# Layer 1's third and fourth quarters as seven half-size products, layer 2's first operands made just ahead of use

## The chip, the cores and the metric

The kernel runs on one core of a Trainium2 chip. The metric is device microseconds (us) of one execution. One execution was also taken with the hardware profiler, and all stretches and waits below come from it.

Five engines work side by side, each on its own list of instructions in order: PE (matrix products, whose weight loads are listed as PEld), DVE and ACT (element-wise work, both can read the products' banks), POOL (element-wise work on SBUF alone) and SP, which here only issues DMAs. An instruction waits until the semaphores that it names have been raised.

## What is computed

Retention attention, then two feed-forward layers on the 2304 tokens that it gives. The attention part is the same before and after, and is left out here:

```python
def _moe_ref(x, w_in, w_out) -> np.ndarray:
    h = x @ w_in
    g = np.maximum(0.01 * h, h)
    return (g @ w_out).astype(np.float32)
...
def _moe2_ref(x, w_in, w_out) -> np.ndarray:
    h = x @ w_in
    alpha = 1.0
    g = np.where(h > 0.0, h, alpha * (np.exp(np.minimum(h, 0.0)) - 1.0))
    return (g @ w_out).astype(np.float32)
...
    x = _moe_ref(x=x, **moe_kwargs)
    return _moe2_ref(x=x, **moe2_kwargs)
```

Tokens are 2304 = 4 blocks of 512 and a small one of 256; the model width is 512, the inner width 2048. Weights arrive as 64-bit floats, and 32-bit accuracy is kept by splitting each operand into a high and a low part and taking three products: high x high, low x high, high x low.

## The kernel before

**The tiling.** Each layer goes through four quarters of the inner width (`q`, 512 wide, four slices `f` of 128). In a quarter the four blocks of 512 tokens are taken one after the other, then the small one. For a block a quarter has a *first product* (x by `w_in`, into banks `ps_h`), the activation, and a *second product* (the result `g` by `w_out`, into four banks `ps_y`), which is added to `yp` in SBUF. A second product is always 4 slices x 4 banks x 3 = 48 matmuls of 512 columns, in four parts of 12, one part for a slice.

**Layer 1, all four quarters.** The first product is plain (`moe_h`): 4 slices x 4 x 3 = 48 matmuls of 512 columns. The work is a list of units (quarter, block, slice); a loop runs over it and takes the second product of a unit three units later (`LAG`). Beside them it splits the weights of the next quarter (`split_a`, `split_b`, `split_c`: two instructions on ACT, four on DVE, then a copy on ACT and a subtraction on DVE or POOL). The table `turn` says at which unit, from 54 on, what else is done.

**Layer 2, all four quarters.** The first product of a block is made as seven half-size ones (`seven`, `seventh`; Strassen's scheme in Winograd's form): 7 x 12 = 84 matmuls of 256 columns, called P1, P2, P5, P3, P6, P7, P4 in their order. Their operands are sums of quarters of x (four tiles for each block, `k` = 0 to 3, name `xo` when loaded back from DRAM and `xs` when just made, always high and low part) and sums of quarters of the weights (`ws`, made on POOL by `sums_a` and `sums_b`). P1, P6, P7 and P4 add into one bank (called `a` in the code), P2 has its own, P5 and P3 share one. Between them the results are read: a copy of a bank by ACT (`k1`, `k5`, `k3`, tile `cc`), then an addition of another bank to it by DVE (`c1`, `c2`, `c3`, tile `c`). So P6 needs `k1` to have read bank `a`, P7 needs `c2`, and P4 needs `c3`. Each of the four results then goes through five steps (ACT, ACT, DVE, ACT copies the high part, DVE subtracts it to get the low part, into `gg`).

The order of all this within a block is a string of tokens, one for each engine's next step (`ORDER`):

```python
        "turn": (
            "f0 P1 k1 aa P2 f1 c1 P5 k5 1 1 ba ba ba ba y s ga 1 ab 1 w P3 f2 k3 P6 c2 1 da 2 2 "
            "bb bb 2 y 2 P7 f3 c3 2 3 3 bb 2 y bb db s s gb 3 P4 4 4 3 4 go y s"
        ),
```

`P` is one of the seven products; `y` is the next waiting part of a second product, here that of the block before, the last `y` the block's own first part; `1` to `4` are the next step of one of the four activations; `f` loads an operand of the next block from DRAM; `a`, `b`, `d` with a letter are the steps of splitting a weight slab; `s` is a step of `stage`; `w` makes a `ws` tile.

**Between the layers.** `stage(blk)` makes the operands of layer 2 out of `yp`: seven high parts on ACT, seven low parts and four differences on DVE, and it sends four tiles to DRAM. Blocks 0 to 2 are staged inside layer 1's last quarter, from units 60, 64 and 70 on, and loaded back; block 3 is staged in layer 2's first blocks and its tiles are used directly.

Of the kernel before, what the change touches and what calls it, by code (L numbers as in the profile page):

```python
# [15 lines left out]
ALU = mybir.AluOpType  # L16
# [20 lines left out]
LAG = 3  # L37

# [15 lines left out]
def _in_order(y, parts):  # L54

    for k in (parts, 1, 1):
        y = y.reshape(k, -1, 2, DM).transpose(0, 2, 1, 3).reshape(-1, DM)
    return y
# [33 lines left out]
def retention_moe(  # L92
# [257 lines left out]
    def split_a(key):  # L350
# [3 lines left out]
        if key[0] == "i" and FT <= key[1] < FT + FQ:  # L354
            u = bpool.tile([P, DM], F32, tag="c", name="u", bufs=6)
        else:
            u = dpool.tile([P, DM], F32, tag="u", name="u", bufs=2)
# [22 lines left out]
    def split_c(key):  # L380

        u = words[key]
        if key[0] == "o" or key[1] < FT or key in added:
            del words[key]
# [4 lines left out]
        engine = nc.gpsimd if key[1] < FQ or key[1] >= FT and key not in early else nc.vector  # L389
# [21 lines left out]
    def moe_h(u):  # L411
# [5 lines left out]
        for i, f in enumerate(fs):  # L417
# [8 lines left out]
            for k, (a, x) in enumerate(ops):  # L426
                product(h[:, i * n : (i + 1) * n], a, x, start=k == 0, stop=k == len(ops) - 1)
# [142 lines left out]
    def evac(m, q, blk, cols, y):  # L570
# [3 lines left out]
        for e in range(len(y)):  # L574
# [12 lines left out]
    units = [  # L587
        (0, q, blk, fs)
        for q in range(NQ)
        for blk in ([0, 1, NMAIN, 2, 3] if q == NQ - 1 else range(NB))  # L590
        for fs in ([(f,) for f in range(FQ)] if blk < NMAIN else [(0, 1), (2, 3)])
    ]
    nsteps = B * STEPS
# [4 lines left out]
        for kind, k in zip(*(("ioioiioo", (0, 0, 1, 1, 2, 3, 2, 3)) if i < FT else ("ooiiiioo", (0, 2, 0, 1, 2, 3, 1, 3))))  # L598
    ]
    early = [("o", FT), ("o", FT + 2)]  # L600
    late = "i16 i17 o14 o15 i18 i19 o16 o18"
    late = [(k[0], int(k[1:])) for k in late.split()]
    at = order.index(("o", FT - 2))
    order = order[:at] + late + order[at + 8 :]
# [13 lines left out]
    def may_split(n):  # L618
# [4 lines left out]
        return i < WB or last_use[kind, min(i, FT + 1) - WB] <= n + (kind == "i")  # L623
# [3 lines left out]
    spilled, operands = {}, {}  # L627

    def stage(blk):

        a = yp.pop(blk)
        assert blk not in yb
# [4 lines left out]
        def room(k, ops=2):  # L637
            where = (big, "big") if blk >= NMAIN - 2 and k % 2 == 0 else (xpool, "x")
            kept[k] = where[0].tile([P, ops, 2, 2, n], F32R, tag=where[1], name="xs")
# [14 lines left out]
        def send(k):  # L654
            t = kept.pop(k)
            d = spill.tile(list(t.shape), F32, tag=f"x{blk}{k}", name=f"x{blk}{k}")
            nc.sync.dma_start(out=d, in_=t.bitcast(F32))
            spilled[blk, k] = d
            if blk == NMAIN - 1:
                operands[blk, k] = t  # L660
# [9 lines left out]
        yield from pair(0, b11, b21)  # L670
        t1 = less(b12, b11)
        yield
        send(0)
        yield from pair(1, t1, b22)
        t2 = less(b22, t1)
        t3 = less(b22, b12)
        yield
        send(1)
        yield from pair(2, t2, t3)
        t4 = less(b21, t2)  # L680
        yield
        send(2)
        yield from pair(3, t4)
        yield
        send(3)
# [22 lines left out]

    def sums_b(key):
        i = key[1]  # L710
        for j in (i, i + 1):
            added.add(("i", j))
            if ("i", j) in weights:
                del words["i", j]
        t = sums[i]
# [9 lines left out]
    def seventh(out, q, blk, j, first=False):  # L725

        n = SIZES[blk] // 2
        x = operands[blk, j // 2][:, j % 2]
        for pair in range(2):
            i = FT + q * FQ + 2 * pair  # L730
# [7 lines left out]
            for kk in range(2):  # L738
                c = slice(kk * P, (kk + 1) * P)
                for a, b in ((0, 0), (1, 0), (0, 1)):  # L740
# [4 lines left out]
                    )  # L745

# [19 lines left out]
    def second_y(q, blk, gg):  # L766

        n = SIZES[blk]
        y = yb[blk] = [bank("y", 4) for _ in range(n // P)]
        order = (0, 2, 1, 3)  # L770
        for f in order:
            wh, wl = weights["o", FT + q * FQ + f]
            gh, gl = (gg[f % 2][:, k, f // 2] for k in range(2))
            for e in range(n // P):
                g = slice(e * P, (e + 1) * P)
                ops = (gh[:, g], wh), (gh[:, g], wl), (gl[:, g], wh)
                for k, (a, x) in enumerate(ops):
                    product(y[e], a, x, start=f == 0 and k == 0, stop=f == FQ - 1 and k == 2)
            if f == FQ - 1:
                evac(1, q, blk, DM, yb.pop(blk))  # L780
            yield

    def small_y(q, gg):
        blk, n = NMAIN, SMALL
        y = yb[blk] = [bank("y", 4) for _ in range(n // P)]
# [446 lines left out]
```

## Time and profile before

| what | value |
|---|---|
| three runs | 809.67, 812.0 and 812.81 us, median 812.0 |
| the profiled execution's own time | 808.98 us |
| its span, first to last instruction | 807.2 us |
| PE, busy share of the span | 99% |
| PE clock granted, in every 20 us but the last | 1.00 |
| DVE, ACT, POOL busy share | 66%, 55%, 19% |

The attention fills the first 140 us or so, together with the first quarter of layer 1; layer 1 goes on to about 438 us, and layer 2 fills the rest. The 1.8 us between the span and the execution's own time lie outside the first and last instruction. Of the views, the page shares out the span by engine, the chain of waits lists what the end was waiting for, piece by piece, the timeline lists instructions in order of time with the idle time ahead of each and what ended it, and the windows give the busy time of each engine in a stretch.

### The profile page before, as it was taken

To read this page: it belongs to the slowest core of one execution; us is meant where nothing else is said; L and a number is where in the kernel's file an instruction comes from. 1 tells how busy PE (TensorE), PEld (TensorE's weight loads), DVE (VectorE), ACT (ScalarE), POOL (GpSimd) and SP (SyncE) were. 2 spreads that over 40 slices of the span, in tenths; PEclk is the share of its full clock that TensorE was granted. 3 is DMA by queue.
4 is the path that set the end of the run, shared out by engine and by line. 5 is a ranking of instruction groups with operands and counts; after the bars stand their busy time and mean duration, and the time that the engine had idled before them with its cause. 6 is when DMAs were issued, how large, how long until landed. Compare 5 with 4: busy or idle time off the path is not lost.

```text
span 807.2 us, 13312 instructions
## 1 busy us (share of the span) xinstructions
PE 795.8 (99%) x5240; PEld 711.2 (88%) x5240; DVE 535.6 (66%) x879; ACT 444.3 (55%) x755; POOL 156.0 (19%) x142
## 2 busy tenths in 40 slices
PE   8899999999999999999999999999999999999998
PEld 5778888888888888888889999999999999999997
DVE  5998962556234762568797788557785877775444
ACT  3465534574234542445666688677675766565442
POOL 2566441000000000004121113221134113410000
PEclk9999999999999999999999999999999999999999
DMA  8994530122001220113369976526663565445512
GB/s 337 329 341 142 193 90 14 53 74 62 23 3 49 79 79 0 43 38 105 94 245 369 397 277 236 233 104 247 248 240 134 222 272 212 175 153 182 213 54 78
DMA packets 34094, 129.97 MB, mean 161 GB/s; under 512 B 4080, under 2 KB 7408, under 8 KB 26736
## 3 DMA queue, kind: packets, MB, share of 16 engines
q1 hardware_dynamic: 33744, 128.99, 44.4%
q8 instruction: 41, 0.67, 0.3%
q14 instruction: 21, 0.17, 0.1%
q10 hardware_dynamic: 288, 0.14, 0.1%
HBM read 109.71 MB, written 19.40 MB: 160 GB/s over the span
## 4 chain that ended last, share of the span: by engine, by line
PE 88%; DMA 3%; issue 3%; DVE 2%; POOL 1%; ACT 1%; SPq 0%; DVEq 0%; POOLq 0%; ACTq 0%
PE ps_y L409 44%; PE ps_h L409 41%; DMA ain<-in_att 2%; PE ps_h L214 1%; PE ps_h L260 1%; DMA raw<-in_moe_out 1%; DMA kn<-in_att 1%; PE ps_h L307 0%; PE ps_h L272 0%; DVE raw L370 0%; POOL wil L390 0%; DVE ain L232 0%; DVE u L377 0%; DVE xt L291 0%; ACT u L358 0%
## 5 line engine op out<-in xcount | busy, mean ns | idle before, releaser
L409 PE MATMUL ps_y<-woh,gg 128*128 128x512 f32 x580 | 183.7, 378 | 0.0
L439 DVE TENSOR_TENSOR gl<-g,gh 128x512 fp32r<-128x512 f32 x64 | 44.7, 699 | 117.4 <-ACT g L433 117.2
L409 PEld LDWEIGHTS ps_y<-woh,gg 128*128 128x128 f32 x580 | 109.7, 190 | 13.5
L432 ACT ACTIVATE gh<-ps_h 128x512 fp32r<-128x512 f32 x64 | 38.3, 598 | 145.1 <-PE ps_h L409 145.0
L409 PE MATMUL ps_y<-gh,woh 128*128 128x512 f32 x288 | 110.8, 385 | 0.4 <-ACT woh L388 0.3
L409 PE MATMUL ps_y<-wol,gg 128*128 128x512 f32 x290 | 109.6, 378 | 0.0
L409 PE MATMUL ps_y<-gl,woh 128*128 128x512 f32 x288 | 109.3, 380 | 0.0
L409 PE MATMUL ps_y<-gh,wol 128*128 128x512 f32 (+1 forms) x288 | 106.1, 368 | 0.7 <-POOL wol L390 0.7
L409 PE MATMUL ps_h<-xh,wil 128*128 128x512 f32 x256 | 97.4, 380 | 1.9 <-POOL wil L390 1.9
L409 PE MATMUL ps_h<-xh,wih 128*128 128x512 f32 x256 | 97.5, 381 | 1.3 <-ACT wih L388 1.0
L409 PEld LDWEIGHTS ps_h<-xo,ws 128*128 128x128 f32 x720 | 86.2, 192 | 1.9 <-DVE c L852 0.4
L409 PE MATMUL ps_h<-xo,ws 128*128 128x256 f32 x720 | 87.8, 275 | 0.0
L390 POOL TENSOR_TENSOR wil<-u,wih 128x512 fp32r<-128x512 f32 x20 | 25.6, 1287 | 295.6 <-ACT wih L388 295.5
L409 PE MATMUL ps_h<-xl,wih 128*128 128x512 f32 x256 | 65.7, 379 | 0.0
L409 PE MATMUL ps_h<-xo,wih 128*128 128x256 f32 x360 | 65.1, 275 | 0.0
L409 PEld LDWEIGHTS ps_y<-gh,woh 128*128 128x128 f32 x288 | 54.5, 189 | 9.1 <-ACT woh L388 1.0
L409 PEld LDWEIGHTS ps_y<-gh,wol 128*128 128x128 f32 x288 | 54.6, 190 | 8.5 <-POOL wol L390 1.1
L852 DVE TENSOR_TENSOR c<-ps_h,cc 128x512 f32<-128x512 f32 x48 | 33.1, 690 | 42.9 <-PE ps_h L409 32.1
L579 DVE TENSOR_TENSOR yp<-yp,ps_y 128x512 f32<-128x512 f32 x96 | 59.7, 685 | 2.4 <-PE ps_y L409 2.4
L409 PEld LDWEIGHTS ps_y<-gl,woh 128*128 128x128 f32 x288 | 54.5, 189 | 7.0
L409 PEld LDWEIGHTS ps_y<-wol,gg 128*128 128x128 f32 x290 | 55.1, 190 | 5.7
L358 ACT ACTIVATE u<-raw 128x512 f32<-128x512 f32 x64 | 54.0, 844 | 9.9 <-DMA raw<-in_moe_in 6.6
(117 smaller groups left out, 1492.7 us busy)
## 6 DMA issues: line engine op xcount, KB each, us to landing
xo<-x SPq DMA_DIRECT2D x45, 1024.0 KB, 6.6
raw<-in_moe_in SPq DMA_DIRECT2D x32, 512.0 KB, 3.5
raw<-in_moe_out SPq DMA_DIRECT2D x32, 512.0 KB, 3.6
x<-xs SPq DMA_DIRECT2D x12, 1024.0 KB, 6.6
ain<-in_att SPq DMA_DIRECT2D x16, 512.0 KB, 6.8
xo<-x SPq DMA_DIRECT2D x15, 512.0 KB, 4.6
ain<-in_att SPq DMA_DIRECT2D x20, 256.0 KB, 7.5
out<-yp SPq DMA_DIRECT2D x17, 256.0 KB, 2.1
```

The source lines that it names most:

```text
L214: nc.tensor.matmul(sc[j][keys[j], pr * n : (pr + 1) * n], t[r, 1, pr * n : (pr + 1) * n], t[r, 0, pr * n : (pr + 1) * n], start=True, stop ...
L260: nc.tensor.matmul(x[half[j], pr * n : (pr + 1) * n], st[b][:, j, pr, :], t[:, 2 * j, pr * n : (pr + 1) * n], start=pr == 0, stop=n < CH, ...
L358: nc.scalar.activation(u, high.bitcast(F32), AF.Abs, scale=2.0**16)
L390: engine.tensor_tensor(l, u, h.bitcast(F32), ALU.subtract)
L409: nc.tensor.matmul(out, w, x, **flags)
L432: nc.scalar.activation(gh, h, AF.Prelu, alpha=0.01)
L439: nc.vector.tensor_tensor(gl, g, gh.bitcast(F32), ALU.subtract)
L579: nc.vector.tensor_tensor(t, t, y[e], ALU.add)
L852: nc.vector.tensor_tensor(t, x, y, ALU.add)
```

## The change

Layer 1's first two quarters stay as they are, as 36 units. Its third and fourth quarter now go through `seven`, as layer 2 does, with the activation `prelu` (ACT, then the high part by ACT and the low part by DVE) in the place of `elu`. Their operands are made by a new function, `stage_first`, during the second quarter: for each block it adds the high and low part of x together again on DVE, takes four differences, splits these into high and low parts, and sends seven operands, each in two parts, to DRAM, 14 DMAs of 256 KB a block. The table `turn` starts at unit 16 now.

Layer 2's operands are no longer staged inside layer 1's last quarter for blocks 0 to 2. Each block's `stage` runs one block ahead of its use: that of block 0 in layer 1's last block (kind `last`), those of blocks 1, 2 and 3 in layer 2's first three blocks (kinds `next`, `turn`, `turn`). The tiles are used directly, and also sent to DRAM for the later quarters. In layer 1's last quarter the small block stands second. Every kind of block has a new token string. `split_c` puts the subtraction of layer 2's first three `i` and `o` slabs on DVE. The columns of `moe_h`'s products are paired in another pattern, and the host puts the rows back accordingly.

```diff
@@
-        engine = nc.gpsimd if key[1] < FQ or key[1] >= FT and key not in early else nc.vector
+        engine = nc.gpsimd if key[1] < FQ or key[1] >= POOLED else nc.vector
@@
-                product(h[:, i * n : (i + 1) * n], a, x, start=k == 0, stop=k == len(ops) - 1)
+                product(h[:, i * n : (i + 1) * n], a, x, 2, start=k == 0, stop=k == len(ops) - 1)
@@
+        if q == NQ - 1 and m == 0:
+            stages.append(stage(blk))
+    PLAIN = 2
     units = [
         (0, q, blk, fs)
-        for q in range(NQ)
-        for blk in ([0, 1, NMAIN, 2, 3] if q == NQ - 1 else range(NB))
+        for q in range(PLAIN)
+        for blk in range(NB)
@@
+    def stage_first(blk):
...
+        def whole(j, t):
+            a = bpool.tile([P, 2, n], F32, tag="c", name="a", bufs=6)
+            h, l = (part(x, j, t).bitcast(F32) for x in (xh, xl))
+            nc.vector.tensor_tensor(a, h, l, ALU.add)
+            return a
...
+        def high(k, x):
+            made[k] = bpool.tile([P, 2, n], F32R, tag="t", name="xs", bufs=3)
+            nc.scalar.activation(made[k], x, AF.Copy)
+
+        def low(k, x, *at):
+            h = made.pop(k)
+            l = bpool.tile([P, 2, n], F32R, tag="t", name="xs", bufs=3)
+            nc.vector.tensor_tensor(l, x, h.bitcast(F32), ALU.subtract)
+            for p, t in enumerate((h, l)):
+                nc.sync.dma_start(out=to[at[0]][:, at[1], p], in_=t.bitcast(F32))
...
@@
+    def prelu(c, g, j, cut):
         t = bpool.tile([P, DM], F32, tag="t", name="t", bufs=3)
-        nc.scalar.activation(t, c, AF.Relu, scale=-1.0)
-        yield
-        nc.scalar.activation(t, t, AF.Exp, scale=-1.0)
-        yield
-        nc.vector.scalar_tensor_tensor(t, t, -1.0, c, ALU.add, ALU.max)
+        nc.scalar.activation(t, c, AF.Prelu, alpha=0.01)
...
@@
+        "last": (
+            "s P1 k1 P2 e P5 k5 s s c1 1 w ga 1 y 1 s 1 P3 p P6 k3 c2 2 1 2 y s P7 s 2 c3 2 2 2 3 "
+            "y w s gb P4 4 3 3 go 4 y 3 4 s"
+        ),
+        "next": (
+            "s P1 k1 e aa s P2 c1 P5 ba s k5 1 ba ba 1 s ab y ba 1 P3 k3 ga 1 P6 c2 1 da 2 bb 2 2 "
+            "bb s 2 P7 c3 2 3 y 3 bb 2 s s bb y db 3 P4 4 gb 4 3 4 go s y"
+        ),
+        "turn": (
+            "s s P1 k1 aa P2 c1 P5 s k5 1 ba ba ba ba ga 1 y ab 1 s P3 1 k3 P6 c2 da 2 2 bb s 1 "
+            "bb 2 y P7 c3 s bb 2 3 bb 2 gb y s db 2 3 3 P4 4 4 p go y s 4 3"
+        ),
...
@@
+            for blk in ((0, NMAIN, 1, 2, 3) if (m, q) == (0, NQ - 1) else range(NB))
...
+            (0, 2): ("regular", "regular", "regular", "hold", "small"),
+            (0, 3): ("head", "head", "bring", "last", "third"),
+            (1, 0): ("next", "turn", "turn", "hold", "small"),
```

On PE, in layer 2's first block from P5 on (`ws` products are P5, P3, P6 and P7; the second product's parts stand as rows of `woh` and `wol`). Before:

```order
L409 MATMUL ps_h<-xo,ws 128x256 x24
L409 MATMUL ps_y<-gh,woh 128x512
L409 MATMUL ps_y<-gl,woh 128x512
L409 MATMUL ps_y<-gh,wol 128x512
...
L409 MATMUL ps_h<-xo,ws 128x256 x12
```

And now:

```order
L408 MATMUL ps_h<-xs,ws 128x256 x12
L408 MATMUL ps_y<-gg,woh 128x512 x2
L408 MATMUL ps_y<-gg,wol 128x512
...
L408 MATMUL ps_h<-xs,ws 128x256 x36
L408 MATMUL ps_y<-gg,woh 128x512 x2
L408 MATMUL ps_y<-gg,wol 128x512
```

Before, P3 and P6 (24 matmuls) were followed by a part of the second product and only then by P7 (12); now P3, P6 and P7 stand in one row of 36.

On DVE, in layer 2's second block from `c3` on (`c` is the addition of a bank, `gg` a low part of an activation, `xs` a low part and `t<-yp,t` a difference of `stage`, `u` a weight slab being put together). Before:

```order
L852 TENSOR_TENSOR c<-ps_h,cc 128x512
L760 TENSOR_TENSOR gg<-t,gg 128x2x256
L375 SCALAR_TENSOR_TENSOR u<-u,raw 128x512
L377 ISA u<-u,last 128x1024
L645 TENSOR_TENSOR xs<-t,xs 128x512
L645 TENSOR_TENSOR xs<-yp,xs 128x512
```

And now:

```order
L943 TENSOR_TENSOR c<-ps_h,cc 128x512
L711 TENSOR_TENSOR xs<-t,xs 128x512 x2
L717 TENSOR_TENSOR t<-yp,t 128x512
L374 SCALAR_TENSOR_TENSOR u<-u,raw 128x512
L376 ISA u<-u,last 128x1024
L838 TENSOR_TENSOR gg<-t,gg 128x2x256
```

The low part of the second activation stood right behind `c3`; now three steps of `stage` and two of a weight slab stand between them.

## Rows read from the trace of the kernel before

**Rows 1.** The page: busy time by engine, then the chain's shares

```profile
PE 795.8 (99%) x5240; PEld 711.2 (88%) x5240; DVE 535.6 (66%) x879; ACT 444.3 (55%) x755; POOL 156.0 (19%) x142
PE 88%; DMA 3%; issue 3%; DVE 2%; POOL 1%; ACT 1%; SPq 0%; DVEq 0%; POOLq 0%; ACTq 0%
```

**Rows 2.** Chain of waits, pieces: start us, length us, what, matmuls

```profile
271.01 2.59 PE ps_h L409 x12
...
567.25 4.02 PE ps_h L409 x36
571.27 2.59 PE ps_y L409 x12
573.86 2.68 PE ps_h L409 x24
```

**Rows 3.** Windows: stretch, length, busy us (instructions) of each engine, clock, DMA share, GB/s

```profile
146.50:376.90 230.40, 230.40 (x1115) 203.41 (x1114) 126.05 (x219) 101.09 (x177) 9.75 (x7) 1.00 0.15 49
...
437.76:457.50 19.74, 19.74 (x134) 18.48 (x132) 16.77 (x28) 12.06 (x21) 1.31 (x2) 1.00 1.01 400
457.50:477.71 20.21, 20.21 (x134) 18.46 (x132) 16.33 (x27) 17.09 (x30) 3.55 (x3) 1.00 0.93 355
...
547.35:567.09 19.74, 19.74 (x134) 18.46 (x132) 14.22 (x23) 13.16 (x23) 3.80 (x4) 1.00 0.72 281
```

**Rows 4.** The page, groups: count, busy us, mean ns of one, idle before

```profile
L409 PE MATMUL ps_h<-xo,ws 128*128 128x256 f32 x720 | 87.8, 275 | 0.0
...
L409 PEld LDWEIGHTS ps_h<-xo,ws 128*128 128x128 f32 x720 | 86.2, 192 | 1.9 <-DVE c L852 0.4
```

**Rows 5.** Timeline of PE in layer 1's last quarter: start us, length us, instruction, idle before

```profile
376.30 1.03 PE L409 MATMUL ps_h<-xl,wih 128*128 128x512 f32 x4
377.67 0.48 PE L409 MATMUL ps_y<-gh,woh 128*128 128x512 f32 x1 [0.35 <-ACT woh L388]
377.99 0.38 PE L409 MATMUL ps_y<-gl,woh 128*128 128x512 f32 x1
378.40 0.48 PE L409 MATMUL ps_y<-gh,wol 128*128 128x512 f32 x1
378.72 0.38 PE L409 MATMUL ps_y<-gh,woh 128*128 128x512 f32 x1
```

**Rows 6.** Timeline of DVE in layer 2's second block: start us, length us, instruction

```profile
462.03 1.29 DVE L760 TENSOR_TENSOR gg<-t,gg 128x512 fp32r<-128x512 f32 x2
463.24 0.69 DVE L852 TENSOR_TENSOR c<-ps_h,cc 128x512 f32<-128x512 f32 x1
463.84 0.52 DVE L370 TENSOR_SCALAR raw<-raw 128x512 uint32<-128x512 uint32 x1
464.25 0.44 DVE L372 TENSOR_SCALAR u<-u 128x512 f32<-128x512 f32 x1
464.72 0.74 DVE L375 SCALAR_TENSOR_TENSOR u<-u,raw 128x512 uint32<-128x512 uint32 x1
465.60 0.69 DVE L377 CUSTOM_DVE_ANT_0 u<-u,last 128x1024 uint16<-128x1024 uint16 x1
466.21 0.68 DVE L754 SCALAR_TENSOR_TENSOR t<-t,c 128x512 f32<-128x512 f32 x1
```

**Rows 7.** The page, DMA issues: count, KB each, median us to landing

```profile
xo<-x SPq DMA_DIRECT2D x45, 1024.0 KB, 6.6
```

**Rows 8.** Timeline of all engines in the same block, around P7

```profile
468.80 0.69 DVE L852 TENSOR_TENSOR c<-ps_h,cc 128x512 f32<-128x512 f32 x1 [1.90 <-ACT cc L857]
...
469.16 0.38 PE L409 MATMUL ps_y<-woh,gg 128*128 128x512 f32 x1
469.36 1.28 POOL L390 TENSOR_TENSOR wol<-u,woh 128x512 fp32r<-128x512 f32 x1 [10.29 <-ACT woh L388]
469.40 1.78 DVE L760 TENSOR_TENSOR gg<-t,gg 128x512 fp32r<-128x512 f32 x1
...
469.54 1.41 PEld L409 LDWEIGHTS ps_h<-xo,ws 128*128 128x128 f32 x12 [0.40 <-DVE c L852]
```

More of the change, by code (lines that the diff above doesn't have):

```diff
@@ L597, in retention_moe @@
         for i in range(FQ, 2 * FT, FQ)
-        for kind, k in zip(*(("ioioiioo", (0, 0, 1, 1, 2, 3, 2, 3)) if i < FT else ("ooiiiioo", (0, 2, 0, 1, 2, 3, 1, 3))))
+        for kind, k in zip(*(("ioioiioo", (0, 0, 1, 1, 2, 3, 2, 3)) if i < PLAIN * FQ else ("ooiiiioo", (0, 2, 0, 1, 2, 3, 1, 3))))
     ]
[L600 to L604, printed above, removed]
     loads, splits = list(order), list(order)
@@ L637, in room @@
         def room(k, ops=2):
-            where = (big, "big") if blk >= NMAIN - 2 and k % 2 == 0 else (xpool, "x")
-            kept[k] = where[0].tile([P, ops, 2, 2, n], F32R, tag=where[1], name="xs")
+            kept[k] = xpool.tile([P, ops, 2, 2, n], F32R, tag="x", name="xs")
         def high(k, i, x):
@@ L779, in second_y, with small_y @@
             if f == FQ - 1:
-                evac(1, q, blk, DM, yb.pop(blk))
+                evac(m, q, blk, DM, yb.pop(blk))
             yield
-    def small_y(q, gg):
+    def small_y(m, q, gg):
         blk, n = NMAIN, SMALL
-        y = yb[blk] = [bank("y", 4) for _ in range(n // P)]
-        last = q == NQ - 1
+        parts = KC if m == 0 else n // P
+        y = yb[blk] = [bank("y", 4) for _ in range(parts)]
+        last = m == 1 and q == NQ - 1
         groups = [(0, 1), (2, 3)] if last else [(f,) for f in range(FQ)]
@@ L890, in seven @@
-    def seven(kind, q, blk, room, rounds, keep, side, begun=None):
+            "s s P1 k1 aa P2 c1 P5 s k5 1 ba ba ba ba ga 1 y ab 1 s P3 1 k3 P6 c2 da 2 2 bb s 1 "
+            "bb 2 y P7 c3 s bb 2 3 bb 2 gb y s db 2 3 3 P4 4 4 p go y s 4 3"
+        ),
+        "small": (
+            "h h h e y h w h h y e y"
+        ),
+        "third": (
+            "h aa ba ba h y ba h ab bb h h ba bb y bb da y h bb db"
+        ),
+        "end": (
+            "h h y h e e w h h y y h"
+        ),
+    }
@@ L894, in seven, with small_unit @@
+    def small_unit(kind, m, q, room, rounds, side):
+        finish()
+        slabs, ops = dict(zip("ab", rounds)), {}
+        gg = room()
+        parts = small_h(m, q, gg)
+        for token in ORDER[kind].split():
+            if token == "h":
+                go(parts, 1)
+            else:
+                beside(token, slabs, ops, side)
+        go(parts)
+        pending.append(small_y(m, q, gg))
+    def seven(kind, m, q, blk, to, room, rounds, side):
         n = SIZES[blk] // 2
-        to = (blk + 1) % NMAIN if (q, blk) != (NQ - 1, NMAIN - 1) else None
@@ L898, in seven @@
         g, banks, copies, acts, ops = [], {}, {}, {}, {}
+        act = elu if m else prelu
         def operand(x):
-            if to is not None and (q, to) != (0, NMAIN - 1):
+            if to is not None:
                 load_x(to, x)
@@ L922, in seven @@
                 y = add_up(banks["b" if x == "1" else "a"], copies.pop({"1": "1", "2": "3", "3": "5"}[x]))
-                acts[int(x)] = elu(y, g, int(x) // 3, lower if x == "1" else upper)
+                acts[int(x)] = act(y, g, int(x) // 3, lower if x == "1" else upper)
             elif op in "1234":
@@ new lines, in retention_moe @@
+        hpool = None
+        for m, q, blk in todo:
+            kind = kinds[m, q][blk]
+            rounds = [splits.pop(0) for _ in range(min(2, len(splits)))] if "aa" in ORDER[kind] else []
+            if blk == NMAIN:
+                small_unit(kind, m, q, room, rounds, side)
+                continue
+            to = blocks.index((m, q, blk)) + 1
+            to = blocks[to] if to < len(blocks) else None
+            if to and to[:2] == (1, 0):
+                to = None
+            seven(
+                kind, m, q, blk, to and to[0] * NMAIN + to[2],
+                room if hpool else first_room, rounds, side,
+            )
+            if not hpool:
+                in_first.close()
+                hpool = ctx.enter_context(
+                    tc.tile_pool(name="hpool", bufs=2, reuse_waits="tile")
+                )
```

311 lines of the change are left out of this document (186 added, 125 removed).

## The prediction

> **What bounds the kernel now.** The page comes first: PE is busy 795.8 of 807.2 us, and the chain that ends last lies to 88% on PE [rows 1]. So I look for PE time that goes and for PE waits that come. The chain's pieces give PE's pace [rows 2]: twelve matmuls of 512 columns take 2.59 us, 0.216 each, and thirty-six of 256 columns 4.02 us, 0.1117 each. The windows then show where PE has no gap at all: in layer 1's second and third quarter (230 us) it is busy for the whole stretch, with DVE at 126 us and POOL at 9.75, and the granted clock is 1.00 [rows 3]. A block of layer 2 thus needs 84 x 0.1117 + 48 x 0.2158 = 9.38 + 10.36 = 19.74 us, and two of the three blocks in the windows take 19.74 us to the hundredth; the third takes 20.21 [rows 3]. PE's pace explains the time to a hundredth wherever it doesn't wait, so the change is to be counted in matmuls and in waits.
>
> **Part 1, fewer columns on PE: -7.8 us.** Four blocks in each of two quarters change their first product from 48 matmuls of 512 columns to 84 of 256. That is 10.36 against 9.38 us, 0.98 us a block, 7.8 us over eight. The small blocks keep their columns. What a half-size matmul pays for its own weight load is in the row already: the 720 of them against `xo` have as many loads, of 192 ns each [rows 4], and still 36 follow one another in 4.02 us.
>
> **Part 2, waits of before that go: -1.4 us.** In layer 1's last quarter PE waited for the high part of a weight slab: four matmuls from 376.30 on would end at 377.16 by the pace of 0.216, and the next starts at 377.67, 0.51 late; those at 377.99, 378.40 and 378.72 come 0.10, 0.19 and 0.10 later than the pace, 0.9 us together [rows 5]. That slab is now split at other places. The second block of layer 2 took 20.21 instead of 19.74 us [rows 3], 0.47 us; its order is replaced. Sum 1.37.
>
> **Part 3, operands for layer 1: 0.** `stage_first` puts 12 DVE instructions a block into the second quarter, 48 in all. At 0.69 us, the mean of an addition of this size [rows 6], that is 33 us in a quarter of some 93 us. DVE was busy 126 of 230 us there [rows 3], 51 of 93, so it would be at 84 of 93 if none overlapped, and the activations that it delays are used three units (15.5 us) later. I take 0. If DVE lagged there by as much as all twelve instructions of a block, 8.3 us, that would still be less than those 15.5. The prelu spares one ACT instruction and one DVE instruction for each activation against `elu`, so blocks of layer 1's third and fourth quarter have a lighter DVE than those of layer 2. Their operands are loaded back on SP's queue, 1 MB in 6.6 us [rows 7]. They go into tiles that P2, P3, P7 and P4 of the block before set free; the last load is issued some 17 us into a block and lands by 24, and P4, which reads it, runs 15.8 us into the next, at 35.5. The cover is 11 us, and more than one whole load; other traffic of that stretch must eat it before PE sees it. I take 0; two uncovered landings would be 13.2 us.
>
> **Part 4, layer 2's first three blocks, new waits: +2.5 us.** Here `stage` of the next block now lies in the same blocks as the splits and activations; before, one block was staged there, now three.
> In kind `next`, P6 and P7 have become adjacent. P7 writes into the bank that `c2` reads, and `c2` needs P6's end. A half-size matmul takes 275 ns from start to end [rows 4] and the next starts after 112, so 0.16 us of drain; then `c2` for 0.69 us, and 0.05 us until P7's weight load starts (`c2` at 468.80, load at 469.54 [rows 8]). That is 0.9 us, once. Before, a part of the second product stood there and hid it.
> In kind `turn`, two blocks, the block's own first part of the second product needs the low part of activation 2. PE comes there after 84 half-size products and 36 of 512 columns, 9.38 + 7.77 = 17.15 us into the block. P7 ends at 72 x 0.1117 + 24 x 0.2158 = 13.22, with the drain 13.4. On DVE stand from there `c3`, three steps of `stage`, the two of the weight slab, then the low part. From starts in [rows 6]: an addition or subtraction occupies DVE for 0.60 us (463.24 to 463.84), the slab's addition 0.88 (464.72 to 465.60), the custom step 0.61; the low part itself takes 0.69. So 13.4 + 4 x 0.60 + 0.88 + 0.61 + 0.69 = 17.98, and PE waits 0.83 us, twice 1.65. Together 2.5 us. The lower end is 0, if the profile's spacing hides a part of DVE's queue; the upper follows from the next part.
>
> **Part 5, DVE beside POOL: +1.6 us.** A low part on DVE took 1.78 us where it began 0.04 us after POOL's subtraction of 1.28 us [rows 8]; alone two such take 1.29 together [rows 6]. So a collision costs 1.09 us of DVE. In the three blocks POOL has ten instructions (two, two, and two with four sums of weights), and the windows of before show three to four instructions of POOL at most in such a block [rows 3]. DVE has no slack to take them: kind `next` has 35 DVE instructions, 27 at 0.60 and 8 of a split at 4.4 together, 20.6 us in a block of 19.74; `turn` has 30, 17.6 us, where before 27 and 28 were busy for 16.3 and 16.8 [rows 3]. The block that I read closely has one collision; I take one in each of the three blocks, and half of their 3.3 us reaching PE, 1.6. The ends are 0 and all ten, 10.9 us.
> [...]
>
> **The sum.** -7.8 - 1.4 + 2.5 + 1.6 = -5.1 us. The profiled execution took 808.98 us, of which 1.8 us lie outside the span; it lies 3.0 us below the median of the three runs. I put the change on both alike: 803.9 us for an execution like the profiled one, 806.9 us against the median of 812.0.
>
> **The rivals.**
> *The whole gain.* DVE keeps up in the three blocks and the new waits stay near 0: -7.8 - 1.4 = -9.2, 802.8 us. For it: the lag at the first part of the second product is 0.8 us, close to nothing. Against it: P7's wait behind P6 has nothing to hide it.
> *Layer 2's turn eats most of it.* DVE carries its lag from `next` into the first `turn`, the lag of 20.6 - 19.74 = 0.9 us adds to each wait, and six collisions instead of three do so in full: 2.5 + 0.9 + 6.5 - 9.2 = +0.7 at its far end, and -3 to -1 with four or five: 809 to 813 us.
> *Slower: POOL holds DVE.* All ten POOL instructions of the three blocks meet a DVE instruction and none is hidden: 2.5 + 10.9 - 9.2 = +4.2, 816.2 us. It decides from seven collisions on that the sign turns (2.5 + 7 x 1.09 = 10.1 against 9.2). For it: DVE is nearly always busy there, so a POOL instruction nearly always meets it. Against it: before, DVE was busy for 85% of the same blocks and lost 0.47 us there.
> *Operands late.* Two loads of layer 1's operands land unhidden: -5.1 + 13.2 = +8.1, 820 us. Against it: the cover of 11 us, and the DMA share of 1.01 in a block of layer 2 that still took 19.74 us [rows 3].
>
> **How the numbers follow.** The forecast, 804.5 to 809, gets 0.52; the whole gain 0.15; the turn that eats most 0.20; POOL holding DVE 0.08; late operands 0.05. About 0.5%, 4 us, is what a measurement of this kernel can tell from no change, so faster means below 807.9: 0.37 of the forecast and the whole gain, 0.52. Same takes the rest of the forecast, 0.15, and the turn, 0.20: 0.35. Slower is what remains, 0.13. The range runs from 802, just under the whole gain, to 812.5, near the far end of the turn; what it leaves out is the two slower cases and little else.
>
> **What would show it.** Right: 4984 matmuls and a PE busy time near 788; blocks of layer 1's last two quarters at 19.74 us; P7 of layer 2's first block waiting some 0.9 us for `c`; in the next two the first `ps_y` of the block's own activation waiting some 0.8 us for DVE's `gg`. Wrong: PE waits for `xo` in layer 1's third quarter (part 3), waits of several us behind DVE in layer 2's first 60 us with DVE instructions stretched beside POOL (part 5), or blocks of layer 1 above 19.74 us (part 1).

## The result and the profile after

The changed kernel took 803.24 us (median of six runs, 802.69 to 805.45) beside 812.25 us for the kernel before: ratio 0.9897, 95% interval 0.9880 to 0.9914, a gain of 7.0 to 9.7 us. The prediction was 806.9 with a range of 802.0 to 812.5. The time lies in the range, but below the 804.5 to 809 of the forecast itself, and close to the rival "the whole gain" (802.8). It did not come there by that rival's road, as the experiments show. The two profiled executions differ by less than the medians: spans of 807.2 and 801.4 us, 5.8 us. Both numbers need a cause.

The page of the changed kernel, PE and the other engines, then the shares of the chain of waits (beside [rows 1]):

```profile
PE 788.7 (98%) x5528; PEld 713.8 (89%) x5528; DVE 586.6 (73%) x951; ACT 467.9 (58%) x795; POOL 179.2 (22%) x158
PE 85%; DVE 5%; DMA 4%; issue 2%; ACT 1%; POOL 1%; SPq 0%; DVEq 0%; POOLq 0%; ACTq 0%
```

PE has 7.1 us less to do, with 288 more matmuls; DVE has 51 us more. Windows of the changed kernel, with the columns of [rows 3]: the plain second quarter with `stage_first` (and the last units of the first quarter), then five blocks, each with 84 half-size products and one second product: layer 1's first such block, kind `bring`, and layer 2's `next`, `turn`, `turn`:

```profile
146.50:249.80 103.30, 103.30 (x504) 91.13 (x503) 84.59 (x136) 53.84 (x97) 11.14 (x9) 1.00 0.59 191
249.80:270.33 20.53, 20.07 (x142) 18.66 (x140) 16.88 (x34) 11.72 (x22) 2.53 (x1) 1.00 0.91 321
389.99:411.33 21.34, 20.01 (x134) 18.38 (x133) 16.00 (x25) 12.05 (x21) 4.82 (x5) 1.00 0.63 246
431.06:451.95 20.89, 20.03 (x134) 18.55 (x132) 20.76 (x35) 15.40 (x27) 2.97 (x2) 1.00 0.59 211
451.95:471.69 19.74, 19.74 (x134) 18.45 (x132) 18.46 (x30) 17.71 (x32) 2.70 (x2) 1.00 0.64 243
471.69:491.45 19.76, 19.76 (x133) 18.37 (x132) 18.75 (x31) 17.93 (x32) 2.73 (x3) 1.00 0.61 236
```

Against the pace of 19.74 us three blocks are long, by 0.79, 1.60 and 1.15 us; every other block behind them keeps the pace. The `turn` blocks, where the prediction put most of its new waits, have none. Between the two profiles the account closes: -7.8 of products, -0.9 and -0.47 of the waits in [rows 5] and [rows 3], +3.56 of the three long blocks, -0.3 in the first 146 us, together -5.9 against 5.8 measured.

The three long blocks, each by the rows of the timeline that end its wait (start us, length us, engine, instruction, idle before). First `next`, where P7 waits for `c2`, as predicted:

```profile
439.43 0.68 DVE L376 CUSTOM_DVE_ANT_0 u<-u,last 128x1024 uint16<-128x1024 uint16 x1
440.04 0.68 DVE L832 SCALAR_TENSOR_TENSOR t<-t,c 128x512 f32<-128x512 f32 x1
440.64 0.68 DVE L943 TENSOR_TENSOR c<-ps_h,cc 128x512 f32<-128x512 f32 x1
441.37 1.60 PE L408 MATMUL ps_h<-xs,ws 128*128 128x256 f32 x12 [0.86 <-DVE c L943]
```

P7 starts 1.02 us later than PE's pace: 0.9 us as costed, and 0.13 us because `c2` stood on DVE at the end of a row of steps without a gap. The first matmuls behind the wait come 0.1 us slower, so PE loses 1.12 us. Then `bring`, where nothing was predicted:

```profile
395.13 1.06 POOL L771 TENSOR_TENSOR sum<-u,sum 128x256 f32<-128x256 f32 x1
396.22 0.79 ACT L357 ACTIVATE u<-raw 128x512 f32<-128x512 f32 x1 [1.64 <-POOL sum L771]
396.90 0.66 ACT L359 ACTIVATE last<-raw 128x512 uint32<-128x512 uint32 x1
397.46 0.58 ACT L948 ACTIVATE cc<-ps_h 128x512 f32<-128x512 f32 x1
398.09 1.16 PE L408 MATMUL ps_h<-xo,ws 128*128 128x256 f32 x8 [1.33 <-ACT cc L948]
```

ACT stood idle for 1.64 us until POOL's last sum had read a slab `u` (there are two); the copy `k5`, which P3 needs, was third in ACT's list behind that. PE lost 1.6 us. And layer 1's first block of half-size products:

```profile
254.28 0.85 ACT L357 ACTIVATE u<-raw 128x512 f32<-128x512 f32 x1
254.54 0.69 DVE L659 TENSOR_TENSOR xs<-t,xs 128x512 fp32r<-128x512 f32 x1
255.03 0.86 ACT L359 ACTIVATE last<-raw 128x512 uint32<-128x512 uint32 x1
255.14 0.69 DVE L943 TENSOR_TENSOR c<-ps_h,cc 128x512 f32<-128x512 f32 x1
255.86 0.63 ACT L815 ACTIVATE t<-c 128x512 f32<-128x512 f32 x1
256.40 0.58 ACT L948 ACTIVATE cc<-ps_h 128x512 f32<-128x512 f32 x1
257.03 1.16 PE L408 MATMUL ps_h<-xo,ws 128*128 128x256 f32 x8 [0.46 <-ACT cc L948]
```

A step of `stage_first` stood ahead of `c1` on DVE, and two steps of a weight slab ahead of the activation on ACT; both were done at about the same time (`c1` at 255.83, the slab's second step at 255.89), and `k5` stood behind the activation. PE lost 0.73 us.

### The profile page after: what moved, and what is told of

It is laid out like the page before. It is cut to its first block, busy times and chain, and to the rows that moved or that the text cites. A ratio compares the mean times of both kernels' runs of the same rounds, so it can differ in the third digit from the quotient of the medians.

```text
span 801.4 us, 14197 instructions
## 1 busy us (share of the span) xinstructions
PE 788.7 (98%) x5528; PEld 713.8 (89%) x5528; DVE 586.6 (73%) x951; ACT 467.9 (58%) x795; POOL 179.2 (22%) x158
## 4 chain that ended last, share of the span: by engine, by line
PE 85%; DVE 5%; DMA 4%; issue 2%; ACT 1%; POOL 1%; SPq 0%; DVEq 0%; POOLq 0%; ACTq 0%
PE ps_y L408 42%; PE ps_h L408 39%; DMA ain<-in_att 2%; DMA x<-xs 2%; PE ps_h L216 2%; PE ps_h L262 1%; DMA kn<-in_att 1%; DVE u L374 1%; DVE yp L578 1%; PE ps_h L309 0%; PE ps_h L274 0%; DVE gl L438 0%; DVE u L376 0%; DVE xs L659 0%; DVE raw L369 0%
## 5 line engine op out<-in xcount | busy, mean ns | idle before, releaser
L408 PE MATMUL ps_y<-gg,woh 128*128 128x512 f32 x288 | 87.0, 380 | 0.0
L408 PEld LDWEIGHTS ps_h<-xo,wih 128*128 128x128 f32 x480 | 76.0, 192 | 1.1
L408 PE MATMUL ps_h<-xo,wil 128*128 128x256 f32 x240 | 66.0, 275 | 0.0
L948 ACT ACTIVATE cc<-ps_h 128x512 f32<-128x512 f32 x72 | 42.7, 593 | 36.2 <-PE ps_h L408 35.7
L408 PEld LDWEIGHTS ps_y<-gg,woh 128*128 128x128 f32 x288 | 52.3, 190 | 6.0
L374 DVE SCALAR_TENSOR_TENSOR u<-u,raw 128x512 uint32<-128x512 uint32 x64 | 56.6, 884 | 1.3
L408 PE MATMUL ps_y<-gg,wol 128*128 128x512 f32 (+1 forms) x160 | 57.2, 358 | 0.0
L408 PE MATMUL ps_y<-gh,woh 128*128 128x512 f32 x144 | 56.0, 389 | 0.1
L838 DVE TENSOR_TENSOR gg<-t,gg 128x512 fp32r<-128x512 f32 x64 | 47.9, 755 | 10.2 <-ACT gg L836 8.7
L408 PE MATMUL ps_y<-gl,woh 128*128 128x512 f32 x144 | 54.6, 379 | 0.0
```

The source lines that it names most:

```text
L374: nc.vector.scalar_tensor_tensor(x, x, 3, high, ALU.logical_shift_left, ALU.bitwise_or)
L408: nc.tensor.matmul(out, w, x, **flags)
L838: nc.vector.tensor_tensor(lo, t, hi.bitcast(F32), ALU.subtract)
L948: nc.scalar.activation(t, x, AF.Copy)
```

## The experiments

**The kernel before again, `before2`: why do the medians differ more than the profiles?** No edit.

> The kernel before, unedited, once more. The two profiles differ by 5.8 us of span (807.2 to 801.4), the medians of the timed runs by 9.0 us. Theory A: the profiled execution of before was an early one of a spread (808.98 beside a median of 812.25), and another profile of the same program takes 811 to 813 us, with 2 to 4 us more of PE waiting somewhere, most likely in the first 146 us, where waits for inputs and for the attention lie. Theory B: a profile of this program is always near 809 us, and the 3 us belong to runs without a profile. Ratio to the kernel before: 1.000.

Measured: ratio 1.000 (0.9989 to 1.0011), and a profile of 811.84 us with a span of 810.0 us. Theory A holds as to the spread, but not as to the place. Layer 2's first two blocks in this profile, and the rows on ACT and PE that made the first one long:

```profile
438.52:459.92 21.40, 20.25 (x134) 18.45 (x133) 16.36 (x27) 11.89 (x20) 1.28 (x1) 1.00 1.00 402
459.92:480.53 20.61, 20.22 (x134) 18.45 (x133) 16.63 (x28) 17.58 (x31) 3.58 (x3) 1.00 0.91 340
```

```profile
447.52 0.63 ACT L642 ACTIVATE xs<-t 128x512 fp32r<-128x512 f32 x1 [2.94 <-DMA x<-xs]
...
450.08 0.59 ACT L857 ACTIVATE cc<-ps_h 128x512 f32<-128x512 f32 x1
...
451.45 1.27 PE L409 MATMUL ps_h<-xo,ws 128*128 128x256 f32 x9 [0.88 <-DVE c L852]
```

They took 21.40 and 20.61 us where the first profile had 19.74 and 20.21 [rows 3]. `stage` of the kernel before wrote its operand tiles in turn and sent each to DRAM; a new one could be written only when the send of an older one had landed. ACT waited 2.94 us for that here, and the copy `k3` stood behind it. In the first profile the same wait was 1.05 us and hidden: the send landed 6.4 us after its issue there, and 8.3 us after it here. So 2.5 us instead of 0.47 lay in these blocks. Some 1.6 us more were lost at 37 us: the granted clock was 0.50 from 36.95 to 40.36 us, and matmuls of 512 columns came about 0.43 us apart instead of 0.216. PE had stood idle for 0.79 and 0.93 us just before; in the first profile two pauses of 0.77 and 0.93 us stood at the same place, and the clock stayed at 1.00. Up to 146 us the second profile had lost 0.8 us against the first, as other waits there were shorter.

**That wait taken away, `before_s`.** In the kernel before, the step of `stage` goes behind `k3`:

```diff
-            "f0 P1 k1 aa P2 f1 c1 P5 k5 1 1 ba ba ba ba y s ga 1 ab 1 w P3 f2 k3 P6 c2 1 da 2 2 "
+            "f0 P1 k1 aa P2 f1 c1 P5 k5 1 1 ba ba ba ba y ga 1 ab 1 w P3 f2 k3 s P6 c2 1 da 2 2 "
```

> The kernel before, with one edit: in kind turn the step of stage that stood behind the block's first waiting part of the second product now stands behind the copy k3. In the second profile of before (810.0 us) ACT waited 2.94 us there for a sent operand tile (x<-xs) to land before it could write the next, the copy k3 stood behind it on ACT, and P7 started 1.05 us late; in the first profile (807.2 us) the same wait was 1.05 us and P7 was on time. Theory (the 3 us by which the medians differ more than the first profiles lie in this wait of ACT, whose length changes from execution to execution, and the changed kernel has no such wait): layer 2's first two blocks of this kernel take 19.74 to 20.0 us each instead of 21.39 and 20.61, and the time falls by 1.5 to 2.5 us, to 809.5 to 810.5. Rival (the 3 us lie in the first 146 us, where the clock fell in the second profile): the time stays within 0.5 us of 812.0.

Measured: 809.26 us beside 812.04, ratio 0.9964 (0.9951 to 0.9977), 2.8 us (1.9 to 4.0). The two blocks:

```profile
437.91:457.65 19.74, 19.74 (x134) 18.46 (x132) 17.01 (x28) 12.71 (x22) 1.77 (x2) 1.00 1.00 397
457.65:477.39 19.74, 19.74 (x134) 18.46 (x132) 16.61 (x25) 16.57 (x29) 3.73 (x3) 1.00 0.93 358
```

The theory holds, by the timed runs: five took 808.19 to 809.32 us, and thirteen of the kernel before 809.42 to 813.41. The profile alone would not show it, as the send landed early in it (6.3 us). One token moved behind another takes 2.8 us off the kernel before, so about that much of the change's 9.0 us is this wait. In the changed kernel the tiles of `stage` are the operands themselves and are not written again in these blocks, and its profile has no wait for such a send between 405 and 530 us.

**Half of the half-size products, `plain3`.** `PLAIN = 3`, and the table `turn` moved by 18 units (the first two steps of its first weight slab by 19):

```diff
-    PLAIN = 2
+    PLAIN = 3
...
-    TURN = 21
+    TURN = 40
...
-            20: ("", "", "ao8 s s"),
-            21: ("s bo8", "", ""),
...
+            38: ("", "", "s s"),
+            39: ("s", "", "ao12"),
...
-        STAGED = (16, 17, 18, 19)
+        STAGED = (34, 35, 36, 37)
```

> The changed kernel, but with three plain quarters in layer 1 instead of two: only the fourth quarter is made of seven half-size products. The table of what is done beside the plain units is moved by one quarter (18 units), all else stays. Theory of the sum: 4840 matmuls, and PE's own time 3.9 us above that of the changed kernel (four blocks at 0.98 us): PE busy 792.6 against 788.7 us, about 807 us. Rival (a half-size product costs as much as a plain one once its operands are paid for, and the gain comes from the other edits): within 1 us of the changed kernel's 803.2 us. The wait of 0.73 us at the first block of half-size products (256 us) should come again, one quarter later.

Measured: 815.59 us, but with a wait of its own. The page, and the row of that wait:

```profile
PE 792.5 (98%) x5384; PEld 711.5 (88%) x5384; DVE 578.1 (71%) x941; ACT 459.0 (57%) x783; POOL 166.1 (20%) x148
```

```profile
292.48 0.48 PE L408 MATMUL ps_y<-gh,woh 128*128 128x512 f32 x1 [3.03 <-DVE yp L578]
```

PE's work is 792.5 us, 3.8 above the changed kernel's where 3.9 was expected, so the term for the products stands, and the rival falls. The time itself says nothing on it. One quarter later the moved table meets the addition of a quarter's result to `yp` on DVE, and PE waits 3.2 us there, which is this experiment's doing. The wait of 0.73 us did not come again at P3; the first block of half-size products waited 0.85 us at P4 for `c3` instead. The profiled execution was the quickest of the ten, 812.85 us; why the median lies 2.7 us above it is not shown (the granted clock was 0.994 to 0.998 in the nine others and 0.999 in this one).

**The order on ACT in the first block, `first_k5`.** `P5 k5 1 f1` in the place of `P5 1 k5 f1`, for that block alone.

> The changed kernel, with one edit: in the first block of half-size products the copy k5 stands ahead of the first activation's step on ACT instead of behind it. In the changed kernel P3 of this block starts 0.73 us late at 257.03 us, because the copy stood on ACT behind the activation, which waited for DVE's c1, and DVE was still at steps of stage_first and at a weight slab. Theory (DVE's lag reaches PE only through this order on ACT): the wait of 0.73 us is gone, and the block takes 19.8 instead of 20.53 us. Rival (ACT itself is late there, by its steps of the weight slab): the copy comes at the same time, and the wait stays above 0.4 us.

Measured: 803.17 us (ratio to before 0.9896); the block takes 19.81 us, and no wait is left in it, nor at P3 in the profiles of the three later kernels with this edit. So the order on ACT is the cause, and the rival's 0.4 us falls. That the lag came from DVE alone is not shown, since `c1` and ACT's own steps ended together. The time is that of the changed kernel (803.24): this profile was 0.5 us later at 146 us, with a clock of 0.50 from 36.84 to 40.25 us, which the changed kernel's first profile did not have. How long the wait is without the edit changes: in five profiles of kernels that are alike up to there it was 0.73, 0.59 (`after_b`), 1.1, 0.04 and 2.1 us. The longest has its cause beside it, on DVE in `pool_twice`:

```profile
251.37 2.19 DVE L660 TENSOR_TENSOR xs<-t,xs 128x512 fp32r<-128x512 f32 x1 [1.03 <-DMA x<-xs]
```

`stage_first` also sends tiles that are written again, and its last steps wait for sends to land: the same trap as in the kernel before, at another place. (That step also took 2.19 us instead of 0.69, beside an instruction of POOL of 2.38 us.)

**Cover for P7, `next_y`.** A `y` moves ahead of P7 in `next`:

```diff
-            "bb s 2 P7 c3 2 3 y 3 bb 2 s s bb y db 3 P4 4 gb 4 3 4 go s y"
+            "bb s 2 y P7 c3 2 3 3 bb 2 s s bb y db 3 P4 4 gb 4 3 4 go s y"
```

> The changed kernel, with one edit: in kind next (layer 2's first block) a waiting part of the second product stands between P6 and P7, and not behind c3. In the changed kernel P7 waited 1.13 us for c2 there. Theory of the prediction (the wait is the drain of P6 and c2's time, and 2.6 us of other products cover it): the block takes 19.75 instead of 20.89 us. Rival (DVE is over-full in this block, 35 instructions and 20.6 us of work in 19.74 us, and the wait only moves to the next product that needs DVE): 0.5 us or more of wait comes back at P4 or at the next y of the same block.

Measured: 804.14 us; the block takes 21.27 us instead of 20.89. P7 no longer waits, but the block's own first part of the second product does, 1.5 us, since DVE came to the addition of the last banks to `yp` only then. (The profile names ACT's copy `woh`, which ended 0.05 us behind the first of these additions; in `three_edits_b`, where the addition stands earlier, this part ran 3 us ahead of that copy, so it does not need it.) The rival holds: DVE's list in this block (20.8 us busy) is the bound, and cover for one wait only moves it.

**When does the second product need activation 2, `turn_late`.** In `turn`, the low part goes behind the step of activation 3:

```diff
-            "bb 2 y P7 c3 s bb 2 3 bb 2 gb y s db 2 3 3 P4 4 4 p go y s 4 3"
+            "bb 2 y P7 c3 s bb 2 3 bb gb y s db 3 3 2 P4 4 4 p go y s 4 3"
```

> The changed kernel, with one edit: in kind turn the low part of activation 2 stands behind the step of activation 3 on DVE instead of ahead of it, so it ends some 2.5 us later, about 20.4 to 20.7 us into the block instead of 17.9. Theory of the prediction (the first own part of the second product, 17.15 us into the block, needs this low part at its first matmul): PE waits 3.3 to 3.6 us in each of the two blocks. Theory after the trace (its first six matmuls read tokens of activation 1 alone, and the first that reads this low part is the ninth, 18.9 us into the block): PE waits 1.5 to 1.9 us in each, at that matmul. Rival (the low part is never what PE waits for there): no wait.

The rows of the first `turn` of this kernel, which begins at 452.16:

```profile
470.82 0.38 PE L408 MATMUL ps_y<-wol,gg 128*128 128x512 f32 x1
471.94 0.68 DVE L838 TENSOR_TENSOR gg<-t,gg 128x512 fp32r<-128x512 f32 x1
472.68 0.70 PE L408 MATMUL ps_y<-woh,gg 128*128 128x512 f32 x2 [1.48 <-DVE gg L838]
```

PE waited 1.64 us here and 2.18 us in the second `turn` (blocks of 21.48 and 22.03 us; one run, 807.44 us), at the ninth matmul of the part. The second theory holds as to the place, with the second wait longer than its 1.5 to 1.9 us; the prediction's falls. In the changed kernel itself the rows at the same place, in the block that begins at 451.95, are:

```profile
469.10 0.38 PE L408 MATMUL ps_y<-woh,gg 128*128 128x512 f32 x1
469.16 0.68 DVE L838 TENSOR_TENSOR gg<-t,gg 128x512 fp32r<-128x512 f32 x1
469.31 0.38 PE L408 MATMUL ps_y<-wol,gg 128*128 128x512 f32 x1
```

The part begins 17.15 us into the block to the hundredth, and the low part ends at 17.89, 0.74 us later, as costed (17.98). PE goes on all the same, as the bank that it fills first belongs to tokens of activation 1.

**POOL's subtraction twice, `pool_twice`.**

```diff
-        engine.tensor_tensor(l, u, h.bitcast(F32), ALU.subtract)
+        for _ in range(2 if POOLED <= key[1] <= FT + 6 else 1):
+            engine.tensor_tensor(l, u, h.bitcast(F32), ALU.subtract)
```

> The changed kernel, but POOL does its subtraction twice for the slabs 19 to 22 of layer 2, the ones split in its first four blocks, which doubles the collisions of DVE and POOL there. In the changed kernel five collisions in the first three blocks lengthened DVE's instructions by about 2.9 us in all. Theory of the prediction (half of what a collision costs DVE reaches PE): 3 more us of DVE, 1.5 us more of PE waits in the three blocks. Theory after the trace (DVE's queue has slack at these places): under 0.3 us more of PE waits in the blocks of kind turn; the time within 0.5 us of 803.2.

Measured: 808.46 us, ratio 0.9963 to before, 5 us above the changed kernel. Its blocks `next`, `turn`, `turn`:

```profile
433.35:455.15 21.80, 20.02 (x133) 18.55 (x132) 21.67 (x34) 15.00 (x26) 6.05 (x4) 1.00 0.54 200
455.15:475.54 20.39, 20.01 (x133) 18.35 (x132) 19.57 (x31) 17.46 (x31) 3.69 (x3) 1.00 0.59 228
475.54:497.90 22.36, 20.28 (x134) 18.29 (x132) 21.06 (x31) 18.05 (x33) 5.63 (x5) 1.00 0.55 212
```

They are 0.91, 0.65 and 2.60 us longer than in the changed kernel, 4.2 us together. Both theories fall, the second worse: there was no slack to speak of. In `next`, `c2` came 1 us later and P7 with it; in the first `turn` the low part of activation 2 was late at the ninth matmul; in the second, ACT came late to `k5`. Five more DVE instructions were lengthened in these blocks, by 0.9 to 1.1 us each, 5.1 us in all, so PE paid for most of it. PE waits in these blocks for DVE, or for ACT after waits of ACT for DVE; no wait for POOL itself stands there.

**The three waits taken away, `three_edits` and `three_edits_b`,** with the changed kernel beside the latter, `after_b`. Beside `first_k5`: in `bring` the slab's start goes behind `k5`, and in `next` the `y` of `next_y` and an earlier addition to `yp`:

```diff
-            "f0 P1 k1 aa P2 f1 P5 k5 ba ba c1 1 1 ba ba ga y 1 1 P3 f2 k3 P6 ab 1 c2 2 2 bb bb y "
+            "f0 P1 k1 P2 f1 P5 k5 aa ba ba c1 1 1 ba ba ga y 1 1 P3 f2 k3 P6 ab 1 c2 2 2 bb bb y "
...
-            "bb s 2 P7 c3 2 3 y 3 bb 2 s s bb y db 3 P4 4 gb 4 3 4 go s y"
+            "bb s 2 y P7 c3 2 3 3 bb 2 y s s bb db 3 P4 4 gb 4 3 4 go s y"
```

> The changed kernel with the three PE waits that it has behind 146 us taken away: k5 ahead of the first activation in the first block of half-size products (0.73 us); in kind bring the two ACT steps of the weight slab behind k5 instead of ahead of it, since the first of them waited for POOL to set a slab free and k5 waited behind it (1.6 us at 396 us); in kind next a part of the second product between P6 and P7, and the addition of the last part to yp four steps earlier on DVE, ahead of two steps of stage (1.13 us). Theory (the three waits are all that separates PE from its pace there): blocks of 19.8, 19.75 and 19.8 us where 20.53, 21.34 and 20.89 stood, the time 3.2 us under the changed kernel's, about 800.0. Rival for the last (the lag of DVE moves on into the next block): 0.5 us or more of wait in the first block of kind turn.

The first try gave 802.35 to 803.61 us in three runs. Its profiled execution took 1662.99 us, with PE at half its pace from end to end (matmuls of 512 columns 0.44 us apart), and gives no block lengths to compare. So it was run again:

> The three edits together, once more: the timed runs of the first try gave 802.35 to 803.61 us where 800.0 was expected, and its profile was of no use. Theory A (the edits take the three waits away, but each gives way to a later one): the profile shows new PE waits of some 2.5 us behind 256, 396 and 440 us. Theory B (the waits are gone, and something outside these blocks takes longer): the blocks take 19.74 to 19.8 us, and the time is lost elsewhere, in the first 146 us.

> The changed kernel, unedited, once more, beside the next one. A second profile shows which of its waits change from execution to execution. Theory: the wait at the first block of half-size products does (0.73, 1.1, 0.04 and 2.1 us in four profiles of kernels that are the same there), those of 1.5 us in kind bring and 1.1 us in kind next do not. Time 803.2, within 1 us.

Measured on the same chip: `after_b` 804.92 us (803.91 to 806.65; ratio to before 0.9923, 0.9900 to 0.9945), `three_edits_b` 802.72 us (802.44 to 803.11; 0.9893). In `after_b` the blocks `bring` and `next` took 21.36 and 20.89 us again, as expected; its first 146 us took 3.4 us more than in the first profile, with a wait of 2.1 us for an input at 8 us and, right behind it, a granted clock of 0.50 from 11.44 to 14.85 us, and its time of 806.65 comes from there. The blocks of `three_edits_b`: first, `bring`, `next`, `turn`, `turn`:

```profile
250.89:270.69 19.80, 19.80 (x141) 18.74 (x140) 16.78 (x33) 11.49 (x22) 2.54 (x1) 1.00 0.94 323
390.35:410.09 19.74, 19.74 (x133) 18.45 (x132) 15.88 (x25) 12.37 (x21) 6.00 (x5) 1.00 0.70 266
429.83:449.57 19.74, 19.74 (x133) 18.45 (x132) 19.25 (x33) 12.59 (x23) 1.69 (x1) 1.00 0.43 161
449.57:471.18 21.61, 20.01 (x133) 18.37 (x132) 19.49 (x32) 20.22 (x36) 3.86 (x3) 1.00 0.75 274
471.18:491.22 20.04, 20.01 (x134) 18.37 (x132) 18.98 (x31) 18.06 (x33) 2.72 (x3) 1.00 0.61 237
```

All three waits are gone, and 2.15 us come back in the blocks behind `next`. Theory A holds in part: what was put off on DVE in `next` is paid in `turn`; what was only set in another order in the first block and in `bring` is not paid at all.

**Two of the three, `two_edits`,** `next` as in the changed kernel:

> The changed kernel with two of the three edits, those in the first block of half-size products (k5 ahead of the first activation) and in kind bring (the slab's two ACT steps behind k5); kind next stays as it is. With all three, the second profile had blocks of 19.80, 19.74 and 19.74 us there, but the block behind next took 21.61 and the one behind that 20.04 us. Theory (only the edit of next is paid for later, since DVE's work is put off there and not taken away): blocks of 19.80, 19.74, 20.89, 19.74 and 19.76 us, so 2.3 us less waiting than the changed kernel, 1.0 us less than with three edits. Rival (the two others are paid for as well): 0.5 us or more of wait in the blocks of kind turn.

Measured: 801.82 us (801.20 to 804.66), ratio to before 0.9888 (0.9870 to 0.9906), span 799.7 us. Its blocks take 19.89, 19.74, 20.84, 19.74 and 19.76 us, so the theory holds, and the rival falls. Its median is 1.4 us below that of the changed kernel's first six runs, which were taken at another time, and the intervals do not tell the two apart; the profile tells which waits are gone. It is the lowest median here.

**And the order on ACT in `turn`, `four_edits`:** the three edits, and `P5 k5 s` for `P5 s k5` in `turn`.

> The three edits, and in kind turn the copy k5 ahead of a step of stage instead of behind it. With three edits P3 of the first turn started 1.87 us late because k5 stood on ACT behind two high parts of stage, which waited for DVE; without them ahead of it ACT would be free for it 1.0 us sooner. Theory (the lag of DVE reaches PE through the order on ACT, as in the first block): the first turn takes 20.6 us or less instead of 21.61, and the second 19.8. Rival (DVE's lag holds PE elsewhere in the same block): above 21.0 us.

Measured: 802.56 us, and blocks of 19.74, 21.32 and 20.18 us for `next`, `turn`, `turn`. P3's wait fell from 1.87 to 0.87 us, by the 1.0 that was expected, but P7 then waited 0.7 us in the same block. The rival holds.

## Why the prediction came out as it did

**Part 1, the products: right.** 7.8 us were forecast; PE's busy time fell by 7.1, and 3.8 of it came back with half of the half-size products gone (`plain3`). The count of 4984 matmuls was a slip: it is 5528, the 5240 of [rows 1] and 8 x 36. Blocks of layer 1's third and fourth quarter keep 19.74 us wherever nothing waits.

**Part 2, waits of before: mis-sized, 1.4 against 3.7 us.** The step that failed took the waits from one profiled execution, and that was a quick one; the text saw that it lay 3.0 us below the median and put the change "on both alike". The 3 us were a hint: they were waits in the very blocks that the change rewrites (`before2`, 2.5 us; `before_s`, 2.8 us), and so went with them.

**Part 3, operands for layer 1: wrong by 0.7 us, right on the loads.** No wait for `xo` is in any profile. The cover of three units holds for plain units (PE was busy for the whole 103.30 us of the window over the second quarter). But the last block's steps of `stage_first` reach into the first block of half-size products, and there no three units stand between DVE, ACT and PE. What that costs changes from execution to execution: in the two profiles that lost most, 1.1 and 2.1 us, ACT waited 0.39 and 1.38 us for a send of `stage_first` to land close before the block; what sets it in the others is not shown.

**Not in the prediction: `bring`, 1.6 us.** The new order of that kind was read for DVE and PE. The wait came through ACT, from a tile that POOL still read.

**Part 4, `next`: right, 1.12 for 0.9 us, but the reason was half of it.** The prediction blamed the missing cover; `next_y` shows that with cover DVE's list is late at the following place.

**Part 4, `turn`: wrong, 0 for 1.65 us.** The time at which the low part ends was right to 0.1 us. The failed step is "needs the low part of activation 2": a part of the second product is twelve matmuls on four banks, and the first two banks belong to the tokens of activation 1. The limit was 18.9 us into the block, not 17.15.

**Part 5, POOL beside DVE: right on DVE in total, at most 0.2 for 1.6 us on PE.** In the three blocks POOL has six subtractions and not ten instructions; its sums begin at the end of the third. Five of them lengthened one DVE instruction each by 0.6 us or so, 3 us together, where three at 1.09, 3.3 us, were forecast. What each cost depends on what DVE did then:

```profile
433.80 1.69 POOL L389 TENSOR_TENSOR wil<-u,wih 128x512 fp32r<-128x512 f32 x1 [3.01 <-ACT wih L387]
434.26 0.68 DVE L943 TENSOR_TENSOR c<-ps_h,cc 128x512 f32<-128x512 f32 x1
434.87 1.02 DVE L369 TENSOR_SCALAR raw<-raw 128x512 uint32<-128x512 uint32 x1
```

The addition of a bank ran its usual 0.68 us beside POOL's subtraction; the step behind it took 1.02 us where 0.42 to 0.56 is usual. The subtraction at 449.29 met four additions of banks to `yp` and lengthened none (2.48 us for four). So not every DVE instruction that meets POOL is lengthened; what decides it is not shown. The prediction put the 1.09 us of one low part on every collision and did not tell DVE's instructions apart.

The step of 1.02 us stands in the row of DVE steps without a gap that ends with `c2` in `next`, so the 0.13 us by which `c2` came late there are, by these rows, this collision's; no run takes it away alone. That no more of the 3 us reached PE was near luck: five more collisions cost 4.2 us (`pool_twice`).

**The sum.** With the measured terms: -7.8 of products, -0.9 and -2.8 of old waits, +3.5 of new ones, -8.0 us; the runs gave -9.0 with an interval of 7.0 to 9.7. About 1 us is not accounted for; it lies inside that interval, and the first 146 us alone moved by 3 us between profiles of one kernel. The forecast of -5.1 met the total of new waits (4.1 for 3.5 us) by misses that cancelled, which was luck (`bring` and the first block had been put at nothing, `turn` and POOL's share did not come), and fell short by the old waits that its profile did not show. In the rival "layer 2's turn" four or five collisions come to -1.4 and -0.4 us by its own terms, not to -3 to -1; only the lower end of that rival rests on it.

## What to carry to other kernels

Where the profiled execution is quicker than the median, ask which wait of it could be longer in the others, first of all a wait for a DMA on an engine that also carries copies which PE needs (1.05 us in one execution here, 2.94 in another); a change that rewrites that place is worth the longer wait. In the list of an engine that works in order, put what PE waits for ahead of steps that wait for somebody else: that cost nothing here (`two_edits`: 19.89 and 19.74 us for the two blocks, and 19.74 and 19.76 for both of kind `turn`), while moving work on a full engine behind a deadline was paid one block later (`three_edits_b`: 21.61 us behind a `next` of 19.74). And cost a late operand against the first matmul that reads that part of the tile, not the first that reads the tile (18.9 us into the block here, not 17.15).

## What was not expected of the hardware

A send of 1 MB to DRAM landed 6.4 us after its issue in one execution and 8.3 us after it in another of the same program, and held ACT for 1.05 and 2.94 us; the two blocks around it took 2.1 us more in the second, more than most edits here moved. Beside a POOL subtraction, DVE's addition of a bank kept its 0.68 us, a step of a weight slab took 1.02 instead of 0.42 to 0.56, and a low part of an activation 1.78 instead of 0.69 [rows 8]. The granted clock fell to 0.50 for 3.41 us behind two pauses of PE of 0.79 and 0.93 us in one execution of the kernel before, and not behind two of 0.77 and 0.93 us at the same place in another.
